# Loading the FFN's first weight in blocks of two row groups and 512 columns instead of four row groups and 256 columns

## The chip, the core and the metric

The kernel runs on one core of a Trainium2 chip. That core has TensorE (matrix products), VectorE, ScalarE and GpSimd (called PE, DVE, ACT and POOL in the profile), SyncE (SP), which here only issues DMAs, and 16 DMA engines. Each engine works through its own list of instructions in order and waits on semaphores for what others produce. The metric is the device time of one execution in microseconds (us); less is better. Before the change it was 227.96 us, the median of five runs (226.95 to 230.28).

## The reference

Attention with a window and a few sink positions is followed by a feed-forward network (FFN) with a swish whose slope is learned for each column:

```python
scores = scale * (q @ k.T)                      # 4 batches, 8 heads, 768 tokens, head size 64
keep = (pos_k < 4) | ((pos_q - pos_k >= 0) & (pos_q - pos_k < 128))
a = softmax(where(keep, scores, -1e9))
x = (a @ v)                                     # heads side by side: [3072, 512]
h = x @ w_in                                    # w_in: [512, 2048]
g = h * (1 / (1 + exp(-beta * h)))              # beta: [2048]
out = g @ w_out                                 # w_out: [2048, 512]
```

All inputs and the output are 32-bit floats in DRAM. The kernel multiplies in bfloat16, so everything that is loaded is also converted once (a cast).

## The kernel before

**Pieces.** The 3072 tokens are cut into eight half-batches of 384 tokens, numbered 0 to 7 (`hb` in the code). Each has four attention units of two heads. For a unit, q and k are transposed (`T`, TensorE, line 651), scores are formed (`SC`, line 735), ScalarE takes the exponential (line 747), GpSimd or VectorE apply the mask (lines 755 to 766), TensorE multiplies with v (`AV`, line 818), VectorE takes reciprocals of the sums (line 822) and normalises (line 824), and the result is transposed into `xT` (`OT`, line 844, then a copy on ScalarE or VectorE). From half-batch 3 on the transposes of q, k and the result are made by DMA instead (lines 634 and 838).

The FFN of a half-batch has 16 chunks of 128 of the 2048 columns. A chunk (`HQ`, written H0, H1, ... here) is four matmuls that accumulate over the four groups of 128 rows of w_in (line 862), a tanh on ScalarE scaled by half of beta (line 867), and a product on VectorE (line 869). The second product (`OQ`, line 882) takes four chunks at a time with w_out.

**Weights.** Sixteen blocks of 512 KB are loaded by `load_w(j)`: blocks 0 to 7 hold w_in, 8 to 15 hold w_out. They pass through six staging buffers `wst` of [128, 1024] floats (three of them lie in the not yet used last third of the buffer `g`, so the profile shows them under that name), and `cast_w(j)` converts each one into `w_in16` or `w_out16`. Block 0 is converted by ScalarE, blocks 1 to 9 by GpSimd, the rest by whichever engine is free. A block of w_in before the change holds 256 columns and all four row groups. A chunk of 128 columns therefore needs one block, and a block serves two chunks: H0 and H1 need block 0 (w0), H2 and H3 need w1, and so on. A block of w_out holds two row groups and all 512 columns, so each partition receives two pieces of 2 KB.

**What sets the order.** The program is first written down as operations with dependencies (`add`: what it reads, what it writes, an estimated duration in ns). For the start of the kernel that order is by hand: the loads of half-batch 0; its attention; then the list `LOADS`, which interleaves weight blocks with the loads of half-batch 1; then the list `early`, `H0 H1 H2 H3 H4 H5 T4 T5 T6 T7 H6 S5 ...`. After that a loop picks the next piece. `arrange` then plans everything again: it walks through time with its own estimates and gives each engine, whenever that is free, the operation that it believes ready first (among several that are ready, the one with the longest chain behind it). TensorE's groups may move forward by at most ten places, and by three after 60 us. The result is a fixed order for each engine. On the chip an engine that meets an operation whose input isn't there yet waits, even where a later one could run.

For DMAs the planner keeps one clock: a transfer with the estimate `ns` occupies it for 1.15 x `ns`, and it is believed landed 1000 ns after that. A w_in or w_out block is booked with 1190, q or k of half-batch 1 with 1950 each, beta with 20. Operations with a `chain` mark keep among each other the order in which they were written down; these are the loads of half-batches 0 to 2, the weight blocks and beta. All of these loads are issued by SP. Beta's load is written just before that of block 2 (line 1077); beta is transposed on TensorE (line 522) and scaled on VectorE (line 524), and each tanh reads the result.

Until the first FFN chunk can start, TensorE's gaps are filled with products of ones (line 1073) that keep it busy and have no other use.

Of the kernel before, what the change touches and what calls it, by code (L numbers as in the profile page):

```python
# [362 lines left out]
def _program(nc, G, sb, ps, q, k, v, w_in, w_out, beta, out):  # L363
    NU = 2 * NPAIR
    NSTG, NX, NV, NT, NE, NON, NG, NTT, NOS, NWS = 2, 2, 3, 12, 7, 5, 3, 3, 4, 6
    NXT = 5
    CUT = 3
    FAST = 1
    NK = NB // 2
# [157 lines left out]


    def load(hb, n, i):

        b, t0, z = hb // 2, hb % 2 * HALF, hb % NSTG
        if n == "v" or hb >= CUT:
            src = {"q": q, "k": k, "v": v}[n][b, :, t0 + i * 128:t0 + (i + 1) * 128, :].rearrange("h p d -> p h d")
            dst, keys, ns = stg[n][z][:, i, :, :], [("stb", n, z, i)], 1000 if hb < 2 else 1092
        else:
            hs = slice(0, H) if i is None else slice(2 * i, 2 * i + 2) if i < 2 else slice(4, H)
            src = {"q": q, "k": k}[n][b, hs, t0:t0 + HALF, :].rearrange("h (p j) d -> p h (j d)", j=NK)
            dst = stg_p[n][z][:, hs, :, :].rearrange("p h j d -> p h (j d)")
            keys = range(4) if i is None else [i] if i < 2 else range(2, 4)
            ns = 620 * len(keys) if hb == 0 else 1950 if hb == 1 else 2080  # L540
            keys = [("stg", n, z, j) for j in keys]
        after = [("stg", n, z, j) for j in range(4)] if hb in range(CUT, CUT + NSTG) and n != "v" else ()
        add("sp", lambda e: e.dma_start(dst, src), ns, w=keys, dma=f"d{n}{z}{'' if i is None else i}", after=after,  # L543
            chain=hb if hb < 3 else None)

    def load_w(j):

        m, h = j // 2, j % 2
        if m < 4:
            src = w_in_src[:, :, j * 256:(j + 1) * 256]  # L550
        else:
            src = w_out_src[:, 2 * (j - 8):2 * (j - 8) + 2, :]
        dst = wst[j % NWS].rearrange("p c f -> p (c f)").rearrange("p (c f) -> p c f", c=4 if m < 4 else 2)
        add("sp", lambda e: e.dma_start(dst, src), 1190, w=[("wst", j % NWS)], dma=f"dw{j % NWS}",  # L554
            chain=2)

    def cast_w(j):
        m, h = j // 2, j % 2
        if m < 4:
            dst = w_in16[:, :, j * 256:(j + 1) * 256]  # L560
        else:
            dst = w_out16[:, 2 * (j - 8):2 * (j - 8) + 2, :]
        src_ = wst[j % NWS].rearrange("p c f -> p (c f)").rearrange("p (c f) -> p c f", c=4 if m < 4 else 2)
        any_of(copies(dst, src_, {"act": 947} if j == 0 else {"gp": 1060} if j < 10 else {"act": 947, "dve": 602, "gp": 1060}), r=[("wst", j % NWS)], w=[("w16", m, h)])
# [289 lines left out]
    def HQ(T_, m):  # L854
# [6 lines left out]
        for c in range(4):  # L861
            add("pe", lambda e, c=c: e.matmul(  # L862
                hp, w_in16[:, c, m * 128:(m + 1) * 128], xT[:, c, t0:t0 + HALF],
                start=(c == 0), stop=(c == 3)), mm_ns(HALF),
                r=[("w16", m // 4, m // 2 % 2), ("xT", c, T_ % NXT)], x=[("B", bs[0])])
        spare_ = [("wst", NWS // 2 + z) for z in range(NWS // 2)] if (T_, m) == (NG - 1, 0) else []
# [39 lines left out]
    x1 = xl(1)  # L906
    LOADS = xl(0) + [0, 1, 2] + x1[:1] + [3] + x1[1:2] + [4, 5] + x1[2:] + list(range(6, 16))
    LOADS += [("f", 1)] + [x for hb in range(2, NSB) for x in xl(hb) + ([("f", hb // 2 + 1)] if hb in (3, 5) else [])]
    CASTS = [(0, n, i) for i in range(4) for n in "qk"] + [(0, "v", c) for c in range(NK)] + [(hb, n, i) for hb in range(1, NSB) for n in "qkv" for i in range(NK)]
    HS = [(T_, m) for T_ in range(NSB) for m in range(NM)]  # L910
    OS = [(0, t, j) for j in range(4) for t in range(3)]
    OS += [(T_, t, j) for T_ in range(1, NSB) for t in range(3) for j in range(4)]
    XPS = [(hb, n, c) for hb in range(CUT, NSB) for n in "qk" for c in range(NK)]
    n_cast, n_w, n_x = [0], [0], [0]
    BACKLOG, AHEAD, MARGIN = 6000, 300, 200

    def head(s):

        i = done[s]
        if s == "T":  # L920
            if i >= 4 * CUT or i - NT + 4 >= units_scored():
                return None
            if n_cast[0] < (2 * i + 2 if i < 4 else 8 + 9 * (i // 4)):
                return None
# [19 lines left out]
        elif s == "AV":  # L944
            if i >= NU or i >= done["OT"] + NON or i >= units_scored() or n_cast[0] < 11 + 9 * (i // 4):
                return None
# [11 lines left out]
        elif s == "H":  # L958
# [3 lines left out]
            if done["O"] < 12 * (T_ - NG + 1) or T_ == NG - 1 and n_w[0] < 16:  # L962
                return None
            t = G.at([("xTu", c, T_) for c in range(4)] + [("w16", m // 4, m // 2 % 2)])
            tb = banks_at(1)
# [15 lines left out]
    def background():  # L981
# [3 lines left out]
        while moved:  # L985
            moved = False
            i = done["load"]
            if i < len(LOADS) and G.dma_free <= now + BACKLOG:
                x = LOADS[i]
                at_hb = CASTS[n_cast[0]][0] if n_cast[0] < len(CASTS) else NSB  # L990
                if isinstance(x, int):
                    if x - NWS < n_w[0]:
                        load_w(x)
                        mark(("win", x), ("wst", x % NWS))
                        done["load"] += 1
                        moved = True
                elif x[0] == "f":
                    load_first(x[1])
                    done["load"] += 1
                    moved = True  # L1000
                elif x[0] - NSTG < at_hb:
                    load(*x)
# [22 lines left out]
            if n_w[0] < 16:  # L1025
                t = G.at([("win", n_w[0])])
                if t is not None and t <= now + AHEAD:
                    cast_w(n_w[0])
                    n_w[0] += 1
                    moved = True  # L1030

    for x in xl(0):
        load(*x)
# [42 lines left out]
    for x in LOADS[9:9 + 13]:  # L1076
        if x == 2:
            beta_load()
        if isinstance(x, int):
            load_w(x)  # L1080
            cast_w(x)
        else:
            load(*x)
            mark(("in",) + x, ("stb" if x[1] == "v" else "stg", x[1], x[0] % NSTG, x[2] or 0))
    for x in CASTS[11:20]:
        cast(*x)
    ring[0] = [7, 6, 5, 4]
    early = "H0 H1 H2 H3 H4 H5 T4 T5 T6 T7 H6 S5 H7 H8 S6 H9 S7 H10".split()
    for x in early:
# [5 lines left out]
        if x[0] == "T":  # L1095
# [3 lines left out]
                OT=4 + sum(x[0] == "R" for x in early), H=sum(x[0] == "H" for x in early), load=22)  # L1099
    n_cast[0], n_w[0] = 20, 8  # L1100
    last = "O"
# [61 lines left out]
```

## Time and profile before

| what | us |
|---|---|
| median of five runs (range) | 227.96 (226.95 to 230.28) |
| the profiled execution | 225.99 |
| its span, first to last instruction | 224.2 |
| TensorE busy | 216.1 |
| ScalarE busy | 148.5 |
| VectorE busy | 138.5 |
| GpSimd busy | 78.7 |

The granted TensorE clock was 1.0 throughout. The span is what the profile divides; the profiled execution's own time is 1.8 us more, which lies around the span. In the first 50 us the 16 DMA engines are busy nearly without a break. Of the 39.86 MB that the kernel moves, the eight w_in blocks make 4.2 MB, in 4096 packets of 1 KB, and the eight w_out blocks 4.2 MB in 2048 packets of 2 KB.

How to read the lines that follow: a row of the order of time has a start and a duration in us, the engine (with a q where it is the engine's issuing queue, not work), the line of the kernel, the operation, what it writes and reads, the shapes, how often it was repeated, and in brackets how long the engine had stood idle and what ended that. The casts of all kinds stand under lines 473 (ScalarE), 475 (GpSimd) and 478 (VectorE), because one helper records them.

### The profile page before, as it was taken

What the parts mean: (1) busy time and instruction counts of PE and PEld (TensorE: products, weight loads), DVE (VectorE), ACT (ScalarE), POOL (GpSimd) and SP (SyncE); (2) the same over time, 40 slices, a digit from 0 to 9 for tenths busy, and PEclk for the clock granted to TensorE, in tenths of its full rate; (3) what the DMA queues carried; (4) which work ended last, traced back from release to release, by engine and by line L of the source; (5) the groups of instructions that cost most, each with busy time, mean ns of one, the idle gap of its engine ahead of it and who ended that gap; (6) DMA issues with size and microseconds to landing.
All of it is one profiled execution on the core that took longest, in us unless ns stands there. A gap on an engine that the chain in (4) does not pass through costs nothing.

```text
span 224.2 us, 4583 instructions
## 1 busy us (share of the span) xinstructions
PE 216.1 (96%) x1802; PEld 124.2 (55%) x1802; DVE 138.5 (62%) x289; ACT 148.5 (66%) x241; POOL 78.7 (35%) x137
## 2 busy tenths in 40 slices
PE   8988988999999999999999999999999999999994
PEld 5765555545556565656555656456555665555541
DVE  2777789857757765769576644658854564633310
ACT  2787997648983886584668865597666936744431
POOL 6375666034560493066004641057003830000000
PEclk9999999999999999999999999999999999999999
DMA  6999989999889996699749988499448032011112
GB/s 171 257 333 362 286 289 400 389 254 224 161 207 202 222 154 175 137 204 246 180 96 227 185 180 190 88 221 237 104 92 184 13 84 69 0 47 50 47 48 94
DMA packets 96077, 39.86 MB, mean 178 GB/s; under 512 B 82024, under 2 KB 92280, under 8 KB 96056
## 3 DMA queue, kind: packets, MB, share of 16 engines
q1 hardware_dynamic: 94376, 34.07, 66.8%
q0 software_dynamic: 1680, 5.51, 7.8%
q8 instruction: 14, 0.23, 0.4%
q14 instruction: 7, 0.06, 0.1%
HBM read 27.37 MB, written 6.29 MB: 150 GB/s over the span
## 4 chain that ended last, share of the span: by engine, by line
PE 76%; DMA 12%; SPq 9%; POOL 1%; issue 1%; ACT 0%
PE P L882 34%; PE P L862 31%; DMA k_stage<-in_k_dram 5%; SPq L543 5%; SPq L554 4%; PE P L735 4%; PE P L818 4%; DMA g<-in_moe_w_out_dram 3%; DMA v_stage<-in_v_dram 3%; PE P L807 1%; PE P L777 1%; PE P L651 1%; POOL w_out L475 0%; POOL k L475 0%; PE P L844 0%
## 5 line engine op out<-in xcount | busy, mean ns | idle before, releaser
L867 ACT ACTIVATE t<-P,hbeta 128x384 f32<-128x384 f32 x128 | 74.0, 583 | 46.2 <-PE P L862 42.2
L869 DVE SCALAR_TENSOR_TENSOR g<-t,P 128x384 bf16<-128x384 f32 x128 | 70.0, 552 | 48.4 <-ACT t L867 44.7
L862 PE MATMUL P<-xT,w_in 128*128 128x384 bf16 x512 | 97.0, 326 | 0.7 <-DVE g L869 0.5
L882 PE MATMUL P<-w_out,g 128*128 128x512 bf16 x384 | 96.2, 379 | 0.0
L862 PEld LDWEIGHTS P<-xT,w_in 128*128 128x128 bf16 x512 | 48.3, 98 | 39.0 <-DVE g L869 1.7
L761 POOL TENSOR_SCALAR_AFFINE_SELECT E<-E 128x512 bf16<-128x512 bf16 x60 | 40.5, 696 | 57.5 <-ACT E L747 57.3
L882 PEld LDWEIGHTS P<-w_out,g 128*128 128x128 bf16 x384 | 36.0, 98 | 35.1 <-DVE g L869 0.8
L747 ACT ACTIVATE E<-P 128x1024 bf16<-128x1024 f32 x44 | 43.2, 1027 | 4.7 <-PE P L735 4.3
L892 POOL DMA_DIRECT2D out_dram<-osb x21 | 11.8, 562 | 47.2 <-ACT osb L473 47.2
L473 ACT ACTIVATE osb<-P 128x512 f32<-128x512 f32 x17 | 10.1, 597 | 12.7 <-PE P L882 12.6
L824 DVE TENSOR_TENSOR onorm<-P,rden 128x384 bf16<-128x384 f32 x32 | 17.8, 558 | 1.1
L818 PE MATMUL P<-vaug,E 128*128 128x65 bf16 x352 | 17.1, 193 | 0.8 <-DVE E L765 0.7
L818 PEld LDWEIGHTS P<-vaug,E 128*128 128x128 bf16 x352 | 15.6, 97 | 2.8 <-DVE E L765 1.1
L735 PE MATMUL P<-qkT 64*128 64x128 bf16 (+1 forms) x288 | 14.4, 230 | 0.1
L735 PEld LDWEIGHTS P<-qkT 64*128 64x128 bf16 x288 | 9.4, 94 | 8.7 <-issue 4.1
L807 PE MATMUL P<-vS,ES 128*128 128x130 bf16 x64 | 12.7, 220 | 0.0
L755 DVE TENSOR_TENSOR E<-E,maskS 128x512 bf16<-128x512 bf16 x16 | 8.2, 513 | 6.8 <-ACT E L747 6.7
L1073 PE MATMUL P<-ones 128*128 128x256 bf16 x60 | 10.4, 331 | 1.1 <-POOL ones L484 1.1
L478 DVE CAST q<-q_stage 128x512 bf16<-128x512 f32 (+1 forms) x15 | 7.3, 501 | 5.0 <-DMA q_stage<-in_q_dram 4.9
L478 DVE CAST vaug<-v_stage 128x512 bf16<-128x512 f32 x16 | 7.7, 488 | 3.1 <-DMA v_stage<-in_v_dram 3.1
L473 ACT ACTIVATE qkT<-P 128x384 bf16<-128x384 bf16 (+1 forms) x12 | 6.4, 574 | 3.6 <-PE P L651 3.5
L1073 PEld LDWEIGHTS P<-ones 128*128 128x128 bf16 x60 | 6.6, 118 | 3.0 <-POOL ones L484 1.1
(58 smaller groups left out, 117.3 us busy)
## 6 DMA issues: line engine op xcount, KB each, us to landing
v_stage<-in_v_dram SPq DMA_DIRECT2D x24, 256.0 KB, 4.7
out_dram<-osb POOLq DMA_DIRECT2D x21, 256.0 KB, 2.9
q_stage<-in_q_dram SPq DMA_DIRECT2D x15, 256.0 KB, 5.3
k_stage<-in_k_dram SPq DMA_DIRECT2D x15, 256.0 KB, 5.0
wst<-in_moe_w_in_dram SPq DMA_DIRECT2D x5, 512.0 KB, 5.3
wst<-in_moe_w_out_dram SPq DMA_DIRECT2D x4, 512.0 KB, 7.9
g<-in_moe_w_out_dram SPq DMA_DIRECT2D x4, 512.0 KB, 7.7
q_stage<-in_q_dram SPq DMA_DIRECT2D x2, 768.0 KB, 8.8
```

The lines of the kernel that those rows point to most:

```text
L473: return lambda e: e.activation(dst, src, AF.Copy, bias=0.0, scale=scale)
L478: return lambda e: e.tensor_copy(dst, src)
L735: add("pe", lambda e, dst=dst, kt=kt, kc=kc, rows=rows, q0=q0, nq=nq, u=u: e.matmul(dst, kt[rows, kc:kc + 128], qkT[rows, u % NT, 0, q0:q0 ...
L747: add("act", lambda e, src=src, dst_=dst_: e.activation(dst_, src, AF.Exp, bias=0.0, scale=SCALE), act_ns(1024), w=[("E", z)] + [("m", z, ...
L761: alts = {"gp": (lambda e, dd=dd, sg=sg: e.affine_select(dd, dd, [[0, 4], [sg, 128]], ALU.is_ge, 0.0, base=min(sg, 0), channel_multiplier= ...
L818: e.matmul(A[:, c0:c0 + D + 1], E[t_ % NE][:, i, hh, :], vaug[vz][:, kb % NK, 2 * hp + hh, :], start=a, stop=o, skip_group_check=True), 31,
L824: add("dve", lambda e: e.tensor_tensor(onorm[on][:, :, :, :].rearrange("p m h d -> p (m h) d"), av[:, :, 0:D], rden[on][:, :].unsqueeze(2) ...
L862: add("pe", lambda e, c=c: e.matmul(hp, w_in16[:, c, m * 128:(m + 1) * 128], xT[:, c, t0:t0 + HALF], start=(c == 0), stop=(c == 3)), mm_ns ...
L867: add("act", lambda e: e.activation(tt[ti][:, :], hp, AF.Tanh, bias=0.0, scale=hbeta[:, m:m + 1]), act_ns(HALF) + 93, r=["hbeta"], w=[("t" ...
L869: add("dve", lambda e: e.scalar_tensor_tensor(gt[T_ % NG][:, m, :], tt[ti][:, :], 1.0, hp, ALU.add, ALU.mult), dve_ns(HALF), r=[("t", ti)] ...
L882: add("pe", lambda e, m=m: e.matmul(P[:, bk, :], gt[T_ % NG][:, m, t * 128:(t + 1) * 128], w_out16[:, m, :], start=(m == 0), stop=(m == NM ...
L1073: G.fill(lambda e: e.matmul(P[:, 7, 0:256].rearrange("p (a b) -> p a b", a=2), ones[:, :], ones[:, :].unsqueeze(1).to_broadcast([128, 2, 1 ...
```

## The change

A block of w_in now holds 512 columns of two row groups, and is loaded in runs of 2 KB. Blocks 2m and 2m+1 together hold column group m: block 2m its row groups 0 and 1, block 2m+1 its row groups 2 and 3. So two blocks serve four chunks, and the third matmul of H0 already needs block 1. The staging buffers, the number of blocks and the casts keep their sizes. The planner's estimate for a w_in block becomes 1080.

The list `LOADS` changes with it: q of half-batch 1 goes ahead of block 2 (and with it ahead of beta, whose load stays tied to block 2). `CH = 4` puts the loads of half-batch 3 under the `chain` mark too. A chunk may be picked in the loop only once both casts of its column group are planned. The parts for `VG` and `WC` (loads issued by GpSimd) are not reached with the values given, and the rewritten conditions on `n_cast` are the old ones in another form.

```diff
+    VG, W2, WC = 99, 1, 99
+    CH = 4
...
     def load(hb, n, i):
...
         add("sp", lambda e: e.dma_start(dst, src), ns, w=keys, dma=f"d{n}{z}{'' if i is None else i}", after=after,
-            chain=hb if hb < 3 else None)
+            chain=hb if hb < CH else None)
...
     def load_w(j):
         m, h = j // 2, j % 2
         if m < 4:
-            src = w_in_src[:, :, j * 256:(j + 1) * 256]
+            src = w_in_src[:, 2 * h:2 * h + 2, m * 512:(m + 1) * 512] if W2 else w_in_src[:, :, j * 256:(j + 1) * 256]
...
-        dst = wst[j % NWS].rearrange("p c f -> p (c f)").rearrange("p (c f) -> p c f", c=4 if m < 4 else 2)
-        add("sp", lambda e: e.dma_start(dst, src), 1190, w=[("wst", j % NWS)], dma=f"dw{j % NWS}",
+        dst = wst[j % NWS].rearrange("p c f -> p (c f)").rearrange("p (c f) -> p c f", c=4 if m < 4 and not W2 else 2)
+        add("sp", lambda e: e.dma_start(dst, src), (1080 if W2 and j < 8 else 1190), w=[("wst", j % NWS)], dma=f"dw{j % NWS}",
             chain=2)
...
     def cast_w(j):
...
-            dst = w_in16[:, :, j * 256:(j + 1) * 256]
+            dst = w_in16[:, 2 * h:2 * h + 2, m * 512:(m + 1) * 512] if W2 else w_in16[:, :, j * 256:(j + 1) * 256]
...
     def HQ(T_, m):
...
-                r=[("w16", m // 4, m // 2 % 2), ("xT", c, T_ % NXT)], x=[("B", bs[0])])
+                r=[("w16", m // 4, c // 2 if W2 else m // 2 % 2), ("xT", c, T_ % NXT)], x=[("B", bs[0])])
...
-    LOADS = xl(0) + [0, 1, 2] + x1[:1] + [3] + x1[1:2] + [4, 5] + x1[2:] + list(range(6, 16))
+    LOADS = xl(0) + [0, 1] + x1[:1] + [2, 3] + x1[1:2] + [4, 5] + x1[2:] + list(range(6, 16))
...
-            t = G.at([("xTu", c, T_) for c in range(4)] + [("w16", m // 4, m // 2 % 2)])
+            t = G.at([("xTu", c, T_) for c in range(4)] + [("w16", m // 4, i_) for i_ in range(2)])
```

## The prediction

> **What bounds the kernel now.** I read the view by stages first: what each engine was busy in four stretches, in microseconds (columns: window, its length, then PE, PEld, DVE, ACT and POOL busy with their instruction counts, the granted clock, the DMA share, GB/s).
>
> ```profile
> 0.00:18.60 18.60, 16.19 (x179) 12.09 (x180) 11.05 (x26) 12.07 (x19) 10.86 (x35) 1.00 0.95 264
> 18.60:60.00 41.40, 38.95 (x337) 22.36 (x336) 32.57 (x66) 32.16 (x55) 19.26 (x24) 1.00 1.05 299
> 60.00:212.00 152.00, 152.00 (x1250) 85.75 (x1251) 93.52 (x196) 101.32 (x163) 48.63 (x79) 1.00 0.69 143
> 212.00:224.20 12.20, 8.94 (x44) 4.01 (x41) 1.32 (x3) 2.95 (x5) 0.00 (x0) 1.00 0.17 65
> ```
>
> TensorE has no idle time from 60 to 212 us. The change acts before that, where TensorE idles 41.40 - 38.95 = 2.45 us after the first FFN chunk. The chain of waits names DMA landings up to 49.5 us (last the k of the half-batch numbered 2, with 11.42 us), but that overstates them: TensorE has other work meanwhile and stands still there for 0.28 us in all. So a load that lands earlier is worth no more than the TensorE gap it closes, and a load that lands later costs what TensorE has no other work for.
>
> Next, the order of time of the queues around the change. SP:
>
> ```profile
> 8.64 1.77 SPq L554 DMA_DIRECT2D wst<-in_moe_w_in_dram  x2
> 10.45 0.54 SPq L1068 DMA_DIRECT2D beta_st<-in_moe_beta_dram  x1
> 11.04 0.42 SPq L554 DMA_DIRECT2D wst<-in_moe_w_in_dram  x1
> 11.50 0.51 SPq L543 DMA_DIRECT2D q_stage<-in_q_dram  x1
> 12.05 1.91 SPq L554 DMA_DIRECT2D g<-in_moe_w_in_dram  x1
> ```
>
> These issue 4 to 9 us ahead of their landings; what holds them is a full DMA queue. So landings follow each other at the speed of the DMA engines. They can be read where POOL waited for them:
>
> ```profile
> 17.45 1.06 POOL L475 TENSOR_SCALAR_AFFINE_SELECT w_in<-wst 128x1024 bf16<-128x1024 f32 x1 [0.58 <-DMA wst<-in_moe_w_in_dram]
> 19.69 0.91 POOL L475 TENSOR_SCALAR_AFFINE_SELECT q<-q_stage 128x512 bf16<-128x512 f32 x1 [1.19 <-DMA q_stage<-in_q_dram]
> 20.98 1.06 POOL L475 TENSOR_SCALAR_AFFINE_SELECT w_in<-g 128x1024 bf16<-128x1024 f32 x1 [0.38 <-DMA g<-in_moe_w_in_dram]
> 23.29 0.91 POOL L475 TENSOR_SCALAR_AFFINE_SELECT k<-k_stage 128x512 bf16<-128x512 f32 x1 [1.25 <-DMA k_stage<-in_k_dram]
> 24.59 1.06 POOL L475 TENSOR_SCALAR_AFFINE_SELECT w_in<-g 128x1024 bf16<-128x1024 f32 x1 [0.39 <-DMA g<-in_moe_w_in_dram]
> 25.96 1.06 POOL L475 TENSOR_SCALAR_AFFINE_SELECT w_in<-g 128x1024 bf16<-128x1024 f32 x1 [0.31 <-DMA g<-in_moe_w_in_dram]
> ...
> 36.09 1.05 POOL L475 TENSOR_SCALAR_AFFINE_SELECT w_out<-g 128x1024 bf16<-128x1024 f32 x1 [0.51 <-DMA g<-in_moe_w_out_dram]
> 37.33 1.31 POOL L475 TENSOR_SCALAR_AFFINE_SELECT w_out<-g 128x1024 bf16<-128x1024 f32 x1 [0.20 <-DMA g<-in_moe_w_out_dram]
> ```
>
> **The new block shape is already in the trace**: w_out's blocks are [128, 2, 512] with 2 KB runs. From start to start, a w_in block takes 20.98 - 19.69 = 1.29, 24.59 - 23.29 = 1.30 and 25.96 - 24.59 = 1.37 us, mean 1.32. A w_out block takes 37.33 - 36.09 = 1.24, and on VectorE, where two casts waited in the same way, 44.66 - 43.33 = 1.33; mean 1.285. The difference is 0.035 us a block, 0.28 us for eight. The packet records give another end: the median packet takes 46 ns for 1 KB and 84 ns for 2 KB, so 512 x 46 / 16 = 1.47 against 256 x 84 / 16 = 1.34 us on 16 engines, 0.13 us a block, 1.04 us for eight. I take 0.035, because consumers wait for landings, and keep 0 and 0.13 as ends.
>
> [...]
>
> **The changed order.** The load order goes from w0 w1 beta w2 q w3 k w4 w5 to w0 w1 q beta w2 w3 k w4 w5 (q, k: those of the half-batch numbered 1). The sum up to w3 is the same, less four blocks' saving (0.14). Now VectorE and TensorE around the first FFN chunk H0:
>
> ```profile
> 16.89 0.56 DVE L824 TENSOR_TENSOR onorm<-P,rden 128x384 bf16<-128x384 f32 x1
> 17.36 0.16 DVE L524 TENSOR_SCALAR hbeta<-P 128x16 f32<-128x16 f32 x1
> 17.55 0.20 DVE L822 RECIPROCAL rden<-P 128x6 f32<-128x6 f32 x1
> ...
> 19.66 1.22 DVE L478 CAST q<-q_stage 128x512 bf16<-128x512 f32 x2 [1.32 <-DMA q_stage<-in_q_dram]
> ```
>
> ```profile
> 18.40 0.34 PE L844 MATMUL P<-ident,onorm 128*128 128x128 bf16 x3 [0.56 <-DVE onorm L824]
> 18.58 4.98 PE L862 MATMUL P<-xT,w_in 128*128 128x384 bf16 x28
> ...
> 24.26 0.28 PE L651 MATMUL P<-ident,k 128*128 128x128 bf16 x2 [0.29 <-POOL k L475]
> ```
>
> Term 1, the stall before H0. H0 waits for the last of four attention units (reciprocal 17.55, normalisation 17.78, transpose 18.40). VectorE stood 1.32 us at the q cast, which shows that the planner believes loads earlier than they come. It books q at 1.15 x 1950 = 2.24 us behind w1, which it now books 2 x 0.127 us earlier; w1's cast started at 15.21, so q is believed ready at about 17.2, ahead of the reciprocal. An engine is given what is believed ready first: I expect one q cast (0.43 us) between the normalisation that ends at 17.45 and the reciprocal. The landing (times from the DMA semaphores): w1 at 15.15, less 0.07, plus q's own 2.25 (17.40 to 19.65) = 17.33. But w2's step, 17.40 - 15.15 = 2.25, was 0.93 over the usual 1.32; a 16 KB instruction packet began at 14.18 and kept one DMA engine for 0.94. That lag passes to whatever follows w1, now q: 18.26. So the reciprocal starts at max(17.45, 17.33 to 18.31) + 0.43 = 17.88 to 18.74 instead of 17.55, +0.33 to +1.19; if the cast isn't placed there, -0.07. I take +1.1, since the packet is fetched in any case. Beta, now behind q, lands near 18.3; its transpose (0.23 us) and the scaling (0.16 us) end by 18.9, before the first tanh (19.70) needs them.
>
> Term 2, what absorbs it. TensorE then does seven chunks and comes to the transposes of k, where it waited for POOL's cast until 24.26. With +1.1 the seven chunks end 24.5, k's cast 24.06: no wait, and the next transposes start at 24.5 + 0.33 = 24.85 instead of 24.38. That is +0.47.
>
> Term 3, both halves of a w_in column group. A chunk now needs two casts, but matmul by matmul: its third matmul, 0.33 us in, is the first to need the second cast. H0: w1's cast ended 16.28, over 2 us ahead. H4 (21.45) needs w3's, 22.05 - 0.14 = 21.91; it starts at 22.5: no wait. H8 (26.12) needs w5's, 27.02 - 6 x 0.035 = 26.81; its third matmul comes at 26.12 + 0.47 + 0.33 = 26.92: no wait, with 0.1 us to spare, and if that cover goes the cost is 0.7 us less any work moved ahead. H12 (33.97) needs w7's, which ended 33.94 and comes 0.28 earlier: nothing.
>
> Term 4, the later stream. ScalarE and VectorE work without a break through 30 to 36 on the scores that follow those transposes, so the +0.47 goes through. At 49.8 to 50.5 the new k lands 0.28 earlier and TensorE comes later: the 0.28 of idle goes. +0.47 - 0.28 = +0.2 at 60 us, and after that TensorE is full and carries it to the end.
>
> Costed at nothing: casts of 2 x 512 instead of 4 x 256 (1.05 against 1.06 us on POOL, off the path), shorter issues (0.37 against 0.42 us on SP, under a full queue), and the third half-batch's loads (numbered 3) tied to a fixed order. Their transposes ended about 69, and the scores that use them start at 73.1; even the three v loads moved ahead of them (2.65 us of SP) stay inside that. If the cover were gone it would be those 2.65.
>
> **Sum.** The profiled execution took 225.99 us (span 224.2 and 1.8 around it); +0.2 makes 226.2. It lies 1.97 below the median of the runs, 227.96, so the forecast against that is **228.2 us**.
>
> **Rivals.** (a) The cast isn't placed ahead, and the packet records are the right price: k lands 0.5 earlier, the gap at 24 closes and the scores start 0.5 earlier, 0.28 more at 50, 0.2 from later weights: -1.0, 227.0. For it: DMA share 1.05 in that stage; against it: the landing rows. (b) Beta's transpose stands on TensorE ahead of the last unit's matmuls (16.99). TensorE would wait for 18.3 with 18.58 - 16.99 = 1.6 us of chain behind it: H0 at 19.9, +1.3, less 0.6 at the k wait, plus a lost cover at H8 of 0.7: +1.4, 229.4. It decides once beta is believed ready before 17.0. (c) The other side by more than 1%: the whole order is planned anew, and 60 to 212, now without a gap, can only lose. Its place is TensorE's queue behind the scores' masks; the price by the stretch before, 2.45 / 41.4 = 5.9% idle; a quarter of that share over 152 us is 2.3 us, 230.3. It decides from one idle us in 66. (d) A lucky order closes nearly all 2.45: 225.6.
>
> **Chances.** Forecast 0.45, (a) 0.21, (b) 0.14, (c) 0.13, (d) 0.07. About 1% (2.3 us) is what a measurement of this kernel can tell from no change: its five runs span 226.95 to 230.28. That scatter moves some 0.06 out of the middle: faster 0.10, same 0.74, slower 0.16. The range leaves out half of (c) and (d): 225.8 to 230.6.
>
> **What would show it.** Right: w_in casts 1.27 to 1.30 us apart after waits; a q cast waiting on VectorE ahead of the last reciprocal and H0's fourth matmul near 20.4 instead of 19.3; no wait of TensorE for k near 24; TensorE full from 60. Wrong: waits at H4 or H8 for w_in's cast, or TensorE gaps after 60 us.

## The result and the profile after

The changed kernel took 229.93 us in the median (227.12 to 233.72); the kernel before 227.78 us (225.76 to 231.79). The ratio is **1.0065, with a 95% interval of 1.0047 to 1.0084**: slower by some 1.5 us. The ratio is smaller than that of the two medians because it sets aside executions more than 1.5% above the fastest of their kernel, and the changed kernel has more of these; why, is shown below. The forecast was 228.2 us in a range of 225.8 to 230.6, so the time lies in the range and within 1% of before, but 1.7 us above the forecast.

The profiled execution of the changed kernel took 227.12 us, its fastest, against 225.99 us before: +1.13 us at a granted clock of 1.00 in both. So the two traces can be compared line by line, and only afterwards comes what they do not show. By stages (columns as before):

```profile
0.00:18.60 18.60, 15.80 (x181) 11.72 (x181) 10.55 (x24) 11.52 (x18) 10.22 (x35) 1.00 0.97 277
18.60:60.00 41.40, 37.68 (x333) 22.20 (x334) 33.08 (x69) 33.62 (x57) 18.90 (x24) 1.00 1.03 299
60.00:212.00 152.00, 151.73 (x1248) 85.47 (x1247) 96.74 (x201) 100.27 (x161) 47.37 (x76) 1.00 0.71 142
212.00:225.40 13.40, 10.10 (x50) 4.60 (x47) 1.66 (x3) 3.54 (x6) 0.00 (x0) 1.00 0.15 59
```

TensorE idles 41.40 - 37.68 = 3.72 us between 18.6 and 60, before 2.45. From 60 to 212 it idles 0.27 us, before nothing. The loss is made early, as expected. SP issues the new order, q first, then beta, then block 2:

```profile
9.96 0.47 SPq L559 DMA_DIRECT2D q_stage<-in_q_dram  x1
10.47 0.71 SPq L1099 DMA_DIRECT2D beta_st<-in_moe_beta_dram  x1
11.22 0.43 SPq L576 DMA_DIRECT2D wst<-in_moe_w_in_dram  x1
```

VectorE, in its order of time around the last normalisation of half-batch 0:

```profile
16.64 0.56 DVE L849 TENSOR_TENSOR onorm<-P,rden 128x384 bf16<-128x384 f32 x1
18.31 0.43 DVE L481 CAST q<-q_stage 128x512 bf16<-128x512 f32 x1 [1.12 <-DMA q_stage<-in_q_dram]
18.65 0.19 DVE L847 RECIPROCAL rden<-P 128x6 f32<-128x6 f32 x1
18.88 0.56 DVE L849 TENSOR_TENSOR onorm<-P,rden 128x384 bf16<-128x384 f32 x1
```

The cast of q stands ahead of the reciprocal and waits 1.12 us for its load. The reciprocal needs nothing of q, but VectorE works in order. It starts at 18.65 instead of 17.55. TensorE's order of time, from beta's transpose on, shows what that does:

```profile
18.50 0.23 PE L525 MATMUL P<-ident,beta_st 16*128 16x16 f32 x1 [0.90 <-DMA beta_st<-in_moe_beta_dram]
19.49 0.34 PE L869 MATMUL P<-ident,onorm 128*128 128x128 bf16 x3 [0.77 <-DVE onorm L849]
19.67 4.33 PE L887 MATMUL P<-xT,w_in 128*128 128x384 bf16 x24
...
24.01 0.46 PE L676 MATMUL P<-ident,k 128*128 128x128 bf16 x3
...
30.30 0.40 PE L760 MATMUL P<-qkT 64*128 64x256 bf16 x6 [0.52 <-ACT E L772]
31.21 0.40 PE L760 MATMUL P<-qkT 64*128 64x128 bf16 x8 [0.52 <-ACT E L772]
32.13 0.40 PE L760 MATMUL P<-qkT 64*128 64x256 bf16 x6 [0.52 <-ACT E L772]
...
38.03 0.27 PE L843 MATMUL P<-vaug,E 128*128 128x65 bf16 x3 [1.01 <-DVE E L790]
```

H0 starts at 19.67 instead of 18.58, +1.09. TensorE now does six chunks, 24 matmuls, ahead of the transposes of k instead of seven, 28, and no longer waits for k at 24. Three new waits of 0.52 us follow, because the planner now puts the scores of two pieces back to back, with no chunk between them, so that TensorE waits for ScalarE's exponentials. At 37.0 it waits 1.01 us for a mask.

How far TensorE is behind can be followed without caring about the order: at each time I added up the columns that it had multiplied (without the products of ones) and compared with when the kernel before had done as many. Both kernels multiply the same columns, 205 us of them. The lag, at times of the kernel before, is 1.09 us at H0, 0.58 at 25, 0.40 at 28, 1.47 at 32, 0.35 at 36, 1.61 at 38, 1.60 at 48, 0.83 from 52 to 60, and 1.16 from 62 to the end. So about 1 us that comes with the scores back to back is there at 32 and gone by 36. In part it is gone because the kernel before stood still itself just ahead of 36, for a mask:

```profile
35.91 0.20 PE L818 MATMUL P<-vaug,E 128*128 128x65 bf16 x1 [0.71 <-DVE E L765]
```

What stays is the stall, less what the waits for k and for a product at 28.7 had cost before, and a loss at 37.

Beside that loss stand later landings. GpSimd, casts of the w_in blocks 2 to 7 and of the first two w_out blocks after them:

```profile
19.66 1.05 POOL L478 TENSOR_SCALAR_AFFINE_SELECT w_in<-wst 128x1024 bf16<-128x1024 f32 x1 [0.40 <-DMA wst<-in_moe_w_in_dram]
20.90 1.05 POOL L478 TENSOR_SCALAR_AFFINE_SELECT w_in<-g 128x1024 bf16<-128x1024 f32 x1 [0.20 <-DMA g<-in_moe_w_in_dram]
...
24.43 1.05 POOL L478 TENSOR_SCALAR_AFFINE_SELECT w_in<-g 128x1024 bf16<-128x1024 f32 x1 [0.31 <-DMA g<-in_moe_w_in_dram]
25.78 1.05 POOL L478 TENSOR_SCALAR_AFFINE_SELECT w_in<-g 128x1024 bf16<-128x1024 f32 x1 [0.30 <-DMA g<-in_moe_w_in_dram]
...
31.67 1.19 POOL L478 TENSOR_SCALAR_AFFINE_SELECT w_in<-wst 128x1024 bf16<-128x1024 f32 x1 [0.47 <-DMA wst<-in_moe_w_in_dram]
33.80 1.05 POOL L478 TENSOR_SCALAR_AFFINE_SELECT w_in<-wst 128x1024 bf16<-128x1024 f32 x1 [0.94 <-DMA wst<-in_moe_w_in_dram]
35.43 1.05 POOL L478 TENSOR_SCALAR_AFFINE_SELECT w_out<-wst 128x1024 bf16<-128x1024 f32 x1 [0.58 <-DMA wst<-in_moe_w_out_dram]
36.65 1.05 POOL L478 TENSOR_SCALAR_AFFINE_SELECT w_out<-g 128x1024 bf16<-128x1024 f32 x1 [0.17 <-DMA g<-in_moe_w_out_dram]
```

Up to w5 a w_in block follows what stands ahead of it by 1.24 (20.90 - 19.66), 1.22 (24.43, after a k cast at 23.21) and 1.35 us, mean 1.27, where it was 1.32: 0.05 us less, the size foreseen. But w6 and w7 landed at 31.6 and 33.7, 0.73 and 1.0 us later than before. The median 2 KB packet took 84 ns between 28 and 31.5 us as everywhere, but the mean there was 117, because 24 of 398 packets took over 0.3 us; what held those up is open. The casts of the two w_out blocks then fall beside VectorE's last masks of half-batch 1, in the row before the wait:

```profile
35.85 2.12 DVE L790 TENSOR_TENSOR E<-E,maskT 128x512 bf16<-128x512 bf16 x2
```

against, in the kernel before,

```profile
36.80 0.94 DVE L765 TENSOR_TENSOR E<-E,maskT 128x512 bf16<-128x512 bf16 x2
```

The same two masks, the last of ten, took 2.12 us instead of 0.94; the last one ended at 37.97, and TensorE's wait with it. Over the whole stretch from 29 to 38 us ten such masks took 7.29 us of VectorE, before 6.04, 0.41 us the shortest, 1.29 the longest. All that took over 0.9 us ran mostly beside a GpSimd cast, but not every mask beside a cast was long: the last one of the kernel before took 0.42 us beside a cast from end to end, and the last two ran beside casts for about four fifths of their time in both kernels. So what made the last two long is not shown, and no run takes it away by itself.

### The profile page after: what moved, and what is told of

The parts are those of the page before. It is cut to its first block, busy times and chain, and to the rows that moved or that the text cites. A ratio compares the mean times of both kernels' runs of the same rounds, so it can differ in the third digit from the quotient of the medians.

```text
span 225.4 us, 4598 instructions
## 1 busy us (share of the span) xinstructions
PE 215.3 (96%) x1808; PEld 124.0 (55%) x1808; DVE 142.0 (63%) x295; ACT 148.9 (66%) x239; POOL 76.5 (34%) x133
## 4 chain that ended last, share of the span: by engine, by line
PE 82%; DVE 5%; SPq 4%; DMA 4%; ACT 3%; issue 0%
PE P L907 36%; PE P L887 35%; PE P L843 4%; DMA q_stage<-in_q_dram 4%; PE P L760 4%; SPq L559 3%; DVE E L790 2%; ACT E L772 2%; PE P L832 1%; DVE g L894 1%; PE P L676 1%; PE P L869 1%; SPq L576 1%; DVE qkT L481 1%; PE P L802 1%; ACT osb L476 1%
## 5 line engine op out<-in xcount | busy, mean ns | idle before, releaser
L786 POOL TENSOR_SCALAR_AFFINE_SELECT E<-E 128x512 bf16<-128x512 bf16 x60 | 41.2, 707 | 56.9 <-ACT E L772 56.3
L476 ACT ACTIVATE osb<-P 128x512 f32<-128x512 f32 x18 | 10.8, 600 | 13.4 <-PE P L907 13.4
L481 DVE CAST q<-q_stage 128x512 bf16<-128x512 f32 (+1 forms) x20 | 10.7, 543 | 8.4 <-DMA q_stage<-in_q_dram 8.4
L780 DVE TENSOR_TENSOR E<-E,maskS 128x512 bf16<-128x512 bf16 x16 | 8.8, 548 | 2.5 <-ACT E L772 2.4
L847 DVE RECIPROCAL rden<-P 128x6 f32<-128x6 f32 x32 | 6.1, 191 | 4.9 <-PE P L843 4.8
L481 DVE CAST k<-k_stage 128x512 bf16<-128x512 f32 (+1 forms) x15 | 8.4, 567 | 0.9 <-DMA k_stage<-in_k_dram 0.8
```

What stands on the lines that cost most here:

```text
L476: return lambda e: e.activation(dst, src, AF.Copy, bias=0.0, scale=scale)
L481: return lambda e: e.tensor_copy(dst, src)
L786: alts = {"gp": (lambda e, dd=dd, sg=sg: e.affine_select(dd, dd, [[0, 4], [sg, 128]], ALU.is_ge, 0.0, base=min(sg, 0), channel_multiplier= ...
```

## The experiments

### The clock that the first profiles didn't show

The first four runs gave an answer to a question that I had not asked. They were chosen to tell apart the run length, beta's place, the scores back to back, and the list of loads.

**Run length alone.** The changed kernel, but every w_in block loaded by two DMAs of 256 columns each, that is in runs of 1 KB; the order is the same.

```diff
-        add("sp", lambda e: e.dma_start(dst, src), (1080 if W2 and j < 8 else 1190), w=[("wst", j % NWS)], dma=f"dw{j % NWS}",
+        def fn(e):
+            if m < 4:
+                return [e.dma_start(dst[:, :, z:z + 256], src[:, :, z:z + 256]) for z in (0, 256)]
+            return e.dma_start(dst, src)
+        fn.two = m < 4
+        add("sp", fn, (1080 if W2 and j < 8 else 1190), w=[("wst", j % NWS)], dma=f"dw{j % NWS}",
```

> The changed kernel with one thing undone: each w_in block is fetched by two DMAs of 256 columns, so that the runs are 1 KB again; the planned order on TensorE, VectorE, ScalarE and GpSimd is the same instruction by instruction. Theory A (the order costs the time, the run length does nearly nothing): POOL's w_in casts 1.29 to 1.37 us apart where they wait, q's cast on VectorE at most 0.2 us later than 18.31, time against the kernel before 1.005 to 1.009, as the changed kernel's 1.0065. Theory B (blocks 6 and 7 landed 0.7 and 1.0 us later than before because of the 2 KB runs, and that costs the time): block 7 lands near 32.7 instead of 33.7 and the ratio falls below 1.003.

Measured: 229.58 us, ratio 1.0054 [1.0020, 1.0088] to the kernel before. The changed kernel's is 1.0065 [1.0047, 1.0084]: the run length makes no difference that this can tell. With runs of 1 KB the kernel is still slower than the kernel before, so the longer run is not the cause, or not the main one, nor does it bring anything that can be measured. It isn't what delays block 7 either: by the DMA semaphores that block landed 36.73 - 31.73 = 5.0 us after the last v of half-batch 1 here, 33.74 - 29.09 = 4.65 in the changed kernel, and 32.74 - 29.61 = 3.13 in the kernel before.

**Beta first.** The changed kernel with beta's load written ahead of q instead of behind it.

```diff
-        if x == 2:
+        if x == x1[0]:
```

> The changed kernel with beta's load moved ahead of q's; blocks and list otherwise as changed. By the plan VectorE then has the last reciprocal ahead of the q cast, and TensorE runs chunk H9 ahead of the scores S5 and keeps chunks between S6 and S7, as in the kernel before. Theory A (two things of the order cost: the stall ahead of H0, and scores S6 and S7 back to back): H0 starts at 18.4 to 18.6 instead of 19.67, no TensorE waits of 0.5 us for ScalarE's exponentials around 30, TensorE idle from 18.6 to 60 at 2.0 to 2.6 instead of 3.7 us, ratio 0.996 to 1.001. Theory C (a chunk that needs two casts, or the block shape itself, is what costs): ratio stays above 1.004.

Measured: 229.96 us, ratio 1.0063 [1.0023, 1.0103]. The expectation failed: VectorE's stall before the last reciprocal did go, and nothing was gained. The profile has two rows that belong together. TensorE before and after H0:

```profile
17.06 0.23 PE L525 MATMUL P<-ident,beta_st 16*128 16x16 f32 x1 [0.70 <-DMA beta_st<-in_moe_beta_dram]
...
18.59 0.28 PE L843 MATMUL P<-vaug,E 128*128 128x65 bf16 x3 [0.93 <-POOL E L786]
...
20.38 5.58 PE L887 MATMUL P<-xT,w_in 128*128 128x384 bf16 x28
```

and the stages around them, 3.41 us each:

```profile
15.29:18.70 3.41, 1.78 (x44) 1.51 (x41) 2.49 (x9) 1.89 (x3) 2.13 (x3) 1.00 1.00 320
18.71:22.12 3.41, 3.17 (x23) 2.01 (x22) 1.02 (x3) 1.72 (x4) 2.48 (x4) 0.50 1.06 388
22.12:25.53 3.41, 3.41 (x23) 2.03 (x22) 2.54 (x6) 2.94 (x6) 1.55 (x3) 1.00 1.08 381
```

In the first stage TensorE was busy 1.78 of 3.41 us; in the next its granted clock was 0.50. The first chunks' matmuls then start 0.32 us apart (20.375, 20.695, 21.015) instead of 0.163. The waits had become two others, for beta and for a mask that GpSimd does after its cast of block 1, and on top of them comes the clock.

In the profiled executions the granted clock is 1.00 or 0.50 in pieces of 3.413 us: half-clock pieces are 18.71 to 22.12 above and 20.59 to 24.00 in the rows further down, and the full-clock stretch lasts 218.453 us in the trace of the kernel before and 221.866 in that of the changed kernel, one piece more. A mean granted clock c over a span s therefore holds (1 - c) x s / 1.707 such half-clock windows, and each timed execution has its mean clock. Pooled by kernel, over all timed executions whose clock is on record (from several chips; the kernel before had 0.49 to 0.52 windows in an execution on each of three):

| half-clock windows in an execution | before: executions, mean us | changed: executions, mean us |
|---|---|---|
| 0 | 58, 227.42 | 10, 228.39 |
| 1 | 32, 228.32 | 27, 229.86 |
| 2 | 9, 230.29 | 10, 230.61 |
| 3 and 4 | none | 7, 232.6 |
| all | 99, 227.97 | 54, 230.09 |
| windows in an execution, mean | 0.51 | 1.33 |

The changed kernel has 0.83 more half-clock windows in an execution. A window goes with 1.24 us (before) and 1.14 us (changed) by a straight line through the executions, so about 1 us of the 2.1 us between the means stands beside the clock, and the rest, 228.39 - 227.42 = 0.97, is there at full clock too. That is the size of the +1.13 us between the two profiled executions, both at full clock. That the windows go with the time doesn't yet show that they cost it; the next experiment tests that. A changed kernel's execution with the half clock, profiled in a later run of the same kernel (ratio there 1.0088 [1.0050, 1.0125]):

> The changed kernel itself once more, beside the others on the same chip. Theory K: 1.0 to 1.7 half-clock stretches of 3.41 us per execution against about 0.5 in the kernel before; among executions without one the difference to the kernel before is 0.4 to 1.0 us, and over all 1.5 to 2.5 us. If the clock plays no part: the same difference in executions with and without.

```profile
13.76:17.17 3.41, 3.28 (x58) 2.70 (x57) 2.21 (x8) 2.76 (x4) 1.84 (x2) 1.00 1.01 339
17.18:20.59 3.41, 1.38 (x21) 1.02 (x20) 1.87 (x7) 1.66 (x4) 1.75 (x4) 1.00 1.06 390
20.59:24.00 3.41, 3.41 (x13) 1.60 (x11) 0.81 (x2) 1.65 (x3) 1.93 (x3) 0.50 1.08 376
24.00:27.42 3.42, 3.17 (x28) 2.04 (x27) 2.82 (x5) 2.79 (x6) 2.53 (x3) 1.00 1.10 272
```

TensorE is busy 1.38 of 3.41 us while the attention of half-batch 0 ends, and gets half the clock for the next 3.41 us. In the profiled executions of this study a half-clock window always followed one with about 1.5 to 2.2 us of idle (windows after the last work aside), that is 43 to 63% of the window. What decides was not settled. The changed kernel's first profile, with waits of 0.90 and 0.77 us at the same place, had 1.40 us of idle in the window from 17.96 and stayed at full clock; and two windows with 1.69 us of idle (from 39.19 with beta first, from 36.22 with the q casts held back, below) were followed by full clock too, though one with 1.47 (the list alone, from 17.41) was followed by half. So the idle time of one window alone doesn't tell. Nor is the place always the same: in the profiles of the scores apart, the list alone, the old list and the kernel before filled, a half-clock window began between 38 and 42 us, behind waits near 36 to 40.

**Filling the gap.** If the clock is what a gap costs on top, products of ones in the gap must bring that part back without shortening any wait. Seven were put ahead of beta's transpose and five ahead of the last transpose of the results.

```diff
+        for name, n in self.more.items():
+            first = groups[self.name[name]][0]
+            at = new.index(first)
+            new[at:at] = [self.one_more() for _ in range(n)]
...
+    G.fill_more(lambda e: e.matmul(P[:, 5, 0:256].rearrange("p (a b) -> p a b", a=2), ones[:, :],
+                                   ones[:, :].unsqueeze(1).to_broadcast([128, 2, 128]), start=True, stop=True),
+                ["ones"], [5], {'beta': 7, ('R', 3): 5})
```

> The changed kernel with the same order and loads; only TensorE gets more of the products of ones that fill gaps: 7 ahead of beta's transpose and 5 ahead of the last result transpose (about 1.3 us of the 1.67 us that it stood idle there). The stall itself stays: H0 near 19.7. Theory K (TensorE's gaps ahead of H0 bring a stretch of 3.41 us at half clock in many executions, 1.7 us each; the changed kernel had 1.33 of them per execution in 42, the kernel before 0.52 in 29): at most 0.9 per execution, time 0.5 to 1.2 us below the changed kernel, ratio to the kernel before 1.000 to 1.004. Theory A (the lost TensorE time itself, not the clock): 1.2 to 1.5 stretches, ratio 1.005 to 1.009.

TensorE before H0, in the filled kernel (L1126 is the new products):

```profile
19.71 0.93 PE L1126 MATMUL P<-ones 128*128 128x256 bf16 x7
20.57 0.23 PE L544 MATMUL P<-ident,beta_st 16*128 16x16 f32 x1
20.73 0.72 PE L1126 MATMUL P<-ones 128*128 128x256 bf16 x5
21.29 0.33 PE L889 MATMUL P<-ident,onorm 128*128 128x128 bf16 x3
21.46 2.71 PE L907 MATMUL P<-xT,w_in 128*128 128x384 bf16 x14
```

In this execution block 1 landed at 17.35 instead of 14.94, and TensorE waited 1.25 us for a mask that stands behind its cast, so H0 is later than the 19.7 that was expected.

Measured: 228.37 us (227.07 to 229.42), 0.17 half-clock windows in an execution instead of 1.33. The mean lies 228.38 - 227.79 = 0.59 us above that of the kernel before on the same chip, where the changed kernel's lies 2.12 above in the pooled table: 1.53 us came back for 1.16 windows, 1.3 us each. The ten filled executions without a window took 228.29 us in the mean, the changed kernel's ten without one 228.39: the filling took the windows away and left the rest as it was. So the clock's part is shown, and what is left is the rest of the loss: the ratio is 1.0051 [1.0023, 1.0079]. The number of windows fell as theory K had it, but the ratio missed its range, 1.000 to 1.004, and lies inside the changed kernel's interval; the gain stands in the means.

**The same in the kernel before.** Its gaps before the first, second and fourth transposes of the results were filled with 3, 3 and 4 products in the same way.

> The kernel before with the gaps ahead of H0 filled in the same way: 3 products of ones ahead of the first result transpose, 3 ahead of the second, 4 ahead of the last (gaps of 0.44, 0.35 and 0.56 us). Theory K: half-clock stretches fall from 0.52 per execution to 0.3 or less, ratio 0.996 to 0.999. Theory A: nothing moves, ratio 0.999 to 1.001.

Measured: 226.94 us, ratio 0.9971 [0.9932, 1.0010], 0.25 half-clock windows instead of 0.49. The mean fell 0.35 us. It points the same way, but the interval reaches 1, so no gain is claimed; and a later kernel with the same filling (the first of the two under "Mended as a whole") had 0.50 windows against 0.51, no fewer.

### The rest of the loss

**Scores apart.** The changed kernel, where the planner is forced to keep a chunk or another piece between the scores, as before.

```diff
+        for later, earlier in [(('S', 5), ('H', 9)), (('S', 6), ('H', 11)), (('S', 7), ('H', 10)), (('S', 7), ('A', 4))]:
+            groups[self.name[later]][0].preds.append(groups[self.name[earlier]][-1])
```

> The changed kernel with its loads as they are; only the planner is told to place H9 ahead of S5, H11 ahead of S6, and H10 and the first half of the attention product ahead of S7, as in the kernel before. The stall ahead of H0 stays. Theory A1 (scores back to back cost about 1.2 of the 1.5 us): H0 still near 19.7, the three waits of 0.52 us around 30 gone, ratio 1.000 to 1.003. Theory A2 (the stall ahead of H0 is what costs): ratio 1.005 to 1.008.

Measured: the three waits of 0.52 us are gone from the profile, but the median is 231.38 us and the ratio 1.0006 [0.9954, 1.0059], which rests on few executions: ten of twelve had half-clock windows (1.5 in the mean). Inconclusive. The reverse was cleaner.

**Scores together in the kernel before.** The order of the changed kernel is forced on the kernel before: scores back to back, everything else as it was.

```diff
+        for later, earlier in [(('H', 9), ('S', 5)), (('H', 10), ('S', 7)), (('H', 11), ('A', 5)), (('A', 4), ('H', 10))]:
+            groups[self.name[later]][0].preds.append(groups[self.name[earlier]][-1])
```

> The kernel before with its loads and blocks; only the planner is told to place S5 ahead of H9, and S6 and S7 ahead of H10, H11 and the attention products, as in the changed kernel. Theory A1: waits of about 0.5 us for the exponentials near 30, TensorE idle from 18.6 to 60 up from 2.45 to 3.5, ratio 1.003 to 1.006. Theory A2: ratio 0.998 to 1.002.

Its TensorE rows show the waits:

```profile
31.60 0.39 PE L739 MATMUL P<-qkT 64*128 64x256 bf16 x6 [0.52 <-ACT E L751]
32.51 0.40 PE L739 MATMUL P<-qkT 64*128 64x128 bf16 x8 [0.52 <-ACT E L751]
33.43 0.40 PE L739 MATMUL P<-qkT 64*128 64x256 bf16 x6 [0.52 <-ACT E L751]
```

Measured: 227.45 us, ratio 0.9997 [0.9966, 1.0028]. TensorE idles 41.40 - 37.75 = 3.65 us from 18.6 to 60 there, and yet the three most visible new waits of the changed kernel cost nothing that can be measured, at most 0.28% or 0.6 us. That agrees with the lag: 1.47 us at 32, 0.35 at 36. What follows got its scores sooner; the kernel before's wait of 0.71 us for a mask on VectorE is 0.38 in this profile.

**The list alone, and the blocks alone.** The new list in the kernel before (the diff), and the old list in the changed kernel (its reverse).

```diff
-    LOADS = xl(0) + [0, 1, 2] + x1[:1] + [3] + x1[1:2] + [4, 5] + x1[2:] + list(range(6, 16))
+    LOADS = xl(0) + [0, 1] + x1[:1] + [2, 3] + x1[1:2] + [4, 5] + x1[2:] + list(range(6, 16))
```

> The kernel before with the new order of loads alone (q ahead of block 2 and of beta); blocks of four row groups with 1 KB runs, the old estimate, one cast per chunk. Theory A (order, not shape): H0 at 19.5 to 20, VectorE waiting for q ahead of the last reciprocal, scores S6 and S7 back to back, ratio 1.005 to 1.010. Theory C (the new block shape is what costs): ratio 0.998 to 1.002.

> The changed kernel with the old order of loads (block 2 and beta ahead of q); blocks of two row groups, 2 KB runs, a chunk that needs two casts, estimate 1080. By the plan H0 is not held up, but S6 and S7 still follow each other. Theory A1 (the scores' order costs): H0 at 18.5 to 18.9, three waits of about 0.5 us for the exponentials near 30, ratio 1.003 to 1.006. Theory A2 (the stall ahead of H0, with the clock that it brings, is what costs): ratio 0.998 to 1.002.

Measured: the list alone 232.67 us in six executions, ratio 1.0177 [1.0123, 1.0232], with 2.17 half-clock windows; the blocks alone 230.81 us, 1.0111 [1.0067, 1.0156], with 1.73. Both lie above every range that was expected. Neither half is better than the whole, and the list alone is clearly worse. So the old list is no cure: with it the plan puts another thing behind the q cast, VectorE's copy of a result into `xT` (its rows):

```profile
21.91 0.43 DVE L481 CAST q<-q_stage 128x512 bf16<-128x512 f32 x1 [2.22 <-DMA q_stage<-in_q_dram]
22.25 0.35 DVE L481 COPY xT<-P 128x384 bf16<-128x384 bf16 x1
```

and TensorE, in the middle of H0:

```profile
19.92 0.65 PE L887 MATMUL P<-xT,w_in 128*128 128x384 bf16 x3
22.66 1.78 PE L887 MATMUL P<-xT,w_in 128*128 128x384 bf16 x5 [2.08 <-DVE xT L481]
```

In the kernels before and after, ScalarE made the copy that H0's fourth matmul waits for. The list isn't the cause by itself. What the stalls in all three have in common is one kind of thing: a q cast on VectorE, placed where the load is believed to have landed, with something behind it that H0 needs.

**The q casts held back.** To the filled kernel the condition is added that the casts of the second half-batch's q come behind the last normalisation.

```diff
-                src, r = stg_p[n][z][:, :, i, :], [("stg", n, z, j) for j in range(4)]
+                src, r = stg_p[n][z][:, :, i, :], [("stg", n, z, j) for j in range(4)] + ([("on", 3)] if hb == 1 and n == "q" else [])
```

> The changed kernel with TensorE's gaps ahead of H0 filled as before (7 and 5 products of ones), and in addition the q casts tied behind the last of the four normalisations, so that VectorE no longer waits for q ahead of them; beta stays behind q. Against the filled one, which had 0.17 half-clock stretches per execution, this isolates the stall itself. If the stall costs what the prediction said (0.5 us at the next transposes): ratio 0.2 to 0.5 of a per cent lower than the filled one's, 1.000 to 1.003. If all of it is absorbed later: no difference, ratio 1.003 to 1.007.

Measured: 229.23 us, ratio 1.0079 [1.0048, 1.0110], against 1.0051 of the filled kernel without it. The stall on VectorE is gone and the time isn't better, an expectation missed. But the run doesn't isolate the stall, as it was meant to: H0 starts at 21.48 in its profile, in the filled one at 21.46. VectorE's last reciprocal now starts at 19.19 without waiting for q, but TensorE comes to the last transpose only after beta's transpose, which waited 0.34 us for its load behind q and started at 20.59, and the five products after it. So what the stall on VectorE costs isn't told by this run. It had 0.50 half-clock windows, and its executions without one took 229.48 us in the mean, those of the filled kernel 228.29: something else in its order costs. The wait for k is there, 0.28 us at 26.0, which Term 2 of the prediction had named as the thing that absorbs the stall; and a later one appears:

```profile
38.09 0.23 PE L851 MATMUL P<-vS,ES 128*128 128x130 bf16 x1 [1.69 <-DVE g L914]
```

**Mended as a whole.** Last, two kernels that should differ by little but the change. First the filled kernel before, with the cast of block 1 held behind the last masks of half-batch 0 on GpSimd (a wait of TensorE of 0.5 to 1.25 us that several profiles show when the first loads come late):

```diff
-... r=[("wst", j % NWS)], w=[("w16", m, h)])
+... r=[("wst", j % NWS)] + ([("m", 3, 0), ("m", 3, 2)] if j == 1 else []), w=[("w16", m, h)])
```

> The kernel before, its gaps ahead of H0 filled (3, 3 and 4 products of ones), and GpSimd's cast of block 1 tied behind the masks of S3: in the traces of several executions block 1 landed 1 to 2 us later than in the first and GpSimd, waiting for it, held up the mask and with it the last attention unit (0.7 to 1.25 us on TensorE). Expected: no wait of TensorE for GpSimd's mask near 17, H0 0.3 to 1 us earlier in late executions, ratio 0.992 to 0.997 (the filled one alone: 0.9971). If the mask isn't what holds H0: 0.996 to 1.000.

then the changed blocks and list with the same, with beta first, the q casts held back and the gaps filled:

> The changed kernel's blocks and list with the order mended: beta ahead of q, q casts behind the last normalisation, block 1's cast behind the masks of S3, gaps ahead of H0 filled (3, 3 and 4). Theory O (the changed kernel is slower by its order and the clock, and the block shape with 2 KB runs neither costs nor gives anything that can be measured): half-clock stretches at most 0.5 per execution, ratio 0.993 to 1.000, and within 0.4% of the mended kernel before. Theory C (a chunk that needs two casts costs by itself): 0.5% or more above the mended kernel before.

Measured: 227.99 us, ratio 0.9971 [0.9929, 1.0014], and 228.16 us, 1.0030 [0.9992, 1.0068]. With the gaps filled and the order mended, the changed blocks come within the uncertainty of the kernel before, and not below it. Against each other the two mended kernels differ by 0.1% in their medians and by 1.0030 / 0.9971, 0.6%, in their ratios, with intervals that overlap: theory O (within 0.4%) and theory C (0.5% or more) are not told apart. TensorE's rows of the mended kernel show two waits that the changed kernel's profile doesn't have:

```profile
22.95 1.80 PE L907 MATMUL P<-xT,w_in 128*128 128x384 bf16 x10 [0.77 <-POOL w_in L496]
...
27.86 1.15 PE L907 MATMUL P<-xT,w_in 128*128 128x384 bf16 x6 [0.36 <-POOL w_in L496]
```

H0 starts at 18.83 there, and H4 and H8 wait 0.77 and 0.36 us for their second block. So blocks that serve four chunks can make TensorE wait, where the changed kernel itself, with the stall before H0, has no such wait. How much of the 1.13 us is the blocks' own price this profile doesn't tell, because block 3 landed at 21.79 in it and at 20.85 in the changed kernel's.

No version beat the kernel before by more than the measurement is uncertain.

## Why the prediction was right, and where its sum was not

**Term 1, the stall, held in mechanism and size.** q was to land at 18.26: its cast started at 18.31. The reciprocal was to start between 17.88 and 18.74: 18.65. H0's fourth matmul was to come near 20.4: 20.42. The lag at H0 was to be 1.1: 1.09. The 16 KB instruction packet that the sum counted on is in this trace too, at 14.40 for 1.05 us; that it is what delayed q is inferred, no run takes it away. What the prediction read as a full DMA queue is a backlog in the trace of the kernel before: when the issue of block 3 ended, at 13.96 us, SP had issued 5.25 MB and 3.30 MB were moved, and the next two issues took 1.80 and 2.81 us without a wait for an engine.

**Term 2 held.** No wait for k at 24, and a lag of 0.58 us at 25 where the sum had 0.47.

**Term 3 held**: no wait for a w_in cast at H4, H8 or H12. The reason given was the margin that the stall gives. The mended kernel agrees with it, with two waits of 0.77 and 0.36 us where the stall is taken out, but its blocks landed later too, so it doesn't show it alone.

**The block's saving held**: 0.05 us from row to row, 0.035 taken; the run of 1 KB pieces shows that it is worth nothing that can be measured.

**Term 4 was mis-sized.** It said that loads landing 0.28 us earlier would close the idle time at 50 us and leave +0.2 at 60. The idle time at 50 did go, and the lag fell from 1.60 to 0.83 between 48 and 52, by more than the 0.28. But it was 1.60 there instead of 0.47: TensorE waited 1.01 us at 37 for two masks that took 2.12 us instead of 0.94, and w6 and w7 came 0.73 and 1.0 us later, not 0.28 earlier. A wait of 0.27 us at 61 came on top. +1.16 at the end instead of +0.2. Which of the waits between 28 and 40 us makes how much of the last 1 us is not settled: the scores back to back make at most 0.6 us of it, as far as the kernel before tells; holding the q casts back didn't bring H0 forward; and the long masks were not taken away by themselves.

**One term was missing.** The sum went by one profiled execution, at a granted clock of 1.00, and took its distance to the median over to the changed kernel: "It lies 1.97 below the median of the runs, 227.96, so the forecast against that is 228.2 us." That step failed: the changed kernel's profiled execution lies 229.93 - 227.12 = 2.81 us below its median. The clock differs between executions of one kernel, and the changed kernel has 1.33 half-clock windows in an execution instead of 0.51, at 1.1 to 1.3 us each; only 10 of 54 executions had none. In the changed kernel the gap of TensorE ahead of H0, which the change lengthens, decides on most of them, as the filling shows. So of the 1.7 us by which the forecast was too low, about 0.9 is Term 4 (227.12 against 226.2) and 0.8 this distance (2.81 against 1.97).

**Luck.** The forecast was +0.2 us, and the medians lie 2.15 apart. That the time still lies in the range owes something to the range's width, 225.8 to 230.6, stretched upward in part for rival (c), and (c) didn't come.

**Rivals.** (b) came half true: beta's transpose did wait 0.90 us on TensorE, but ahead of the last transpose, where VectorE's stall ran beside it, not ahead of the last unit's products. (c) didn't come: 0.27 us of idle from 60 to 212. (a) and (d) didn't come. `CH = 4` and the block's other casts were costed at nothing, and no run tests that.

## What to carry to other kernels

In a kernel whose order is planned ahead and worked through in order, a load that is issued earlier moves its consumer earlier too, on whatever engine that is; look at what stands behind the consumer, and whether the load really lands when the planner believes. A gap on TensorE in front of the long part of a kernel may cost more than its length (here 1.1 to 1.3 us for each half-clock window), so compare the granted clock of every execution and not only of the profiled one, and fill such gaps with products where that costs nothing. A wait that the trace shows isn't yet a loss: forcing three waits of 0.52 us into the kernel before changed its time by nothing that could be measured.

## What the hardware did that I had not expected

- TensorE's clock was halved for windows of 3.413 us after windows in which it had idled 1.5 to 2.2 us; a half-clock window went with 1.1 to 1.3 us of the time, and filling the gaps brought that back. Windows with as much as 1.69 us of idle were followed by full clock, so what decides is open.
- How often that happens differs by execution of one and the same kernel. The profiles also differ in when the first loads land (the cast of block 1 started between 14.95 and 17.73 in all versions, at 15.00 and 16.21 in two executions of the changed kernel), and with that in where TensorE's gaps are; whether that is the cause was not tested.
- Masks of one shape took 0.41 to 1.29 us on VectorE, those over 0.9 us mostly beside GpSimd casts; but one took 0.42 beside a cast from end to end.
- Packets of 2 KB took 84 ns in the median, also between 28 and 31.5 us, where their mean was 117 because 24 of 398 took over 0.3 us.
